# Softmax denominators of 98 attention units: turned by a DMA transpose and added up on VectorE, with PV ten slots behind

## The chip, the core and the metric

The kernel runs on one core of one Trainium2 chip. A core has TensorE (PE in the profile; its weight loads are PEld), VectorE (DVE), ScalarE (ACT), GpSimd (POOL), SyncE (SP, which here only issues transfers) and 16 DMA engines that all issuing engines share. The time is the device time of one execution in microseconds; several runs give a median.

## The reference

Inputs are bf16. `x` has 2048 tokens of width 512; attention has 32 heads of width 128 over a cache of 2048 keys and values.

```python
xn = layernorm(A_x)                                   # 2048 x 512
# attention: 32 heads, q from xn, keys and values from the cache
q = (xn @ wq) per head                                # 32 x 2048 x 128
p = softmax(q @ k_cache^T * 128**-0.5)                # 32 x 2048 x 2048
s = (p @ v_cache, heads side by side) @ wo            # 2048 x 512
# mixer and MLP on the same xn
h  = gelu(layernorm(xn) @ w1)
x1 = xn + shifted(h) @ w2      # four groups of columns, shifted by -1, +1, -2, +2 tokens
g  = silu(x1 + gelu(layernorm(x1) @ w3) @ w4)         # w3: 512 x 1792
out = A_x + s * g
```

## The kernel before

**Units and slots.** The attention is cut into 128 units: one head (`hh`, four to a group `g`) with one block of 512 queries (`qt`), in the order group, query block, head (`units`). A unit is eight slots. In slot p, `s_slot` computes the scores of two chunks of 128 keys (two matmuls of 512 columns into `ps_s`, keys on the partitions, queries along the columns) and ScalarE's exponential (line 194) writes them as bf16 into half of a `pT` tile; a tile holds two slots, and there are four. `pv_slot` runs `LAG` = 5 slots later and adds two matmuls, V times the exponentials, to the unit's accumulator `ps_o` in PSUM (`psO`, two buffers). So every slot issues two score matmuls and two PV matmuls, and other matmuls are put between them: Q of the unit after next in slots 0 and 1 (`q_mm`, copied out by `q_copy` in slot 2), the output projection of one block of 128 tokens in slots 4 and 5 (`wo_mm`, added into `s_acc` by `wo_post` in slot 6), and the mixer and MLP, cut into 136 chunks, in slots 2 and 3 and in slots 6 and 7, spread evenly from window 10 on. The mixer's first GEMM with its gelu (`m1_chunk`) takes about units 5 to 18, its second (`m2_chunk`) units 19 to 32, and then the wide MLP follows in four rounds of `m3_chunk` (gelu) and `m4_chunk` (silu).

**Denominators.** The softmax needs, for each query, the sum of the exponentials over all 2048 keys. VectorE adds a unit's four `pT` tiles: `add_first` in slot 4, `add_next` in slot 6, and in slot 0 of the next unit `add_last`, which adds the last tile and then folds the four 512-wide parts into one (lines 205, 210, 211). What remains, `acc[:, 0, :]`, has 128 partial sums per query, one per partition. `sums` in slot 3 adds across partitions on TensorE: four matmuls with `acc` as weights and a column of ones as data give a 128x4 tile in PSUM, query 4p+j at partition p, column j. VectorE's reciprocal (`recip`, line 233) writes `rc`; SP stores it to DRAM as `dr` (line 235, 16 contiguous bytes per partition); in slot 4 `bcast` (line 250) reads it back, repeated on all 128 partitions, into `rb` (`rp`, two buffers); and in slot 2 of the unit after, `norm` (line 261) multiplies `ps_o` by `rb` into `oT` and frees the accumulator.

**What sets the order.** The loop over slots writes the order out by hand, and `pin` keeps it on each engine. Each engine, and each issuing queue, works in order: what waits holds up all that is behind it. `todo` holds work for later slots (gelu steps, loads). SP issues the stores and broadcasts above, the loads of K (as transposes), V and weights, and the transposes of normalized tokens; POOL issues the loads and stores of the MLP. Tags with fixed numbers of buffers limit how far transfers run ahead: `ta` and `tb` for token tiles, `w3` for the weights of the wide MLP. PSUM has one bank with the tag `xa` (Q, sums, WO in turn) and one with `xm` (the MLP; late in the run also the sums).

**The ends.** The last group defers two token blocks of the group before it (`deferred`), and the last seven units (`QUIET`) are arranged apart; the last unit's sums are made in parts after the loop (`split_sums`).

Of the kernel before, what the change touches and what calls it, by code (L numbers as in the profile page):

```python
# [9 lines left out]
ALU = mybir.AluOpType  # L10
FP32 = mybir.dt.float32
BF16 = mybir.dt.bfloat16
# [5 lines left out]
def kernel(  # L18
# [70 lines left out]
    wqp = ent(pool("wqp", HG + 2))  # L89
    wop = ent(pool("wop", 2 * HG))  # L90
    qtp = ent(pool("qt", 4))
    ptp = ent(pool("pt", 4))
    trp = ent(pool("tr", 2))
    rp = ent(pool("rp", 2))
    otp = ent(pool("ot", 2))
    smp = ent(pool("smp", 4))
    gtp = ent(pool("gt", 2))
# [26 lines left out]
    LQ = QT - 1  # L124
    deferred = {(NG - 2, qt): qt for qt in (LQ - 1, LQ)}
    NS = NU * SPU
    kTs, vBs, wqs, wos, oTs, st = {}, {}, {}, {}, {}, {}
    todo = defaultdict(list)

    def at(n, fn):  # L130
        todo[n].append(fn)
# [42 lines left out]

    def q_copy(u):
        qT = qtp.tile([P, 512], BF16, name="qT")
        if u > QUIET + 1:
            pin(nc.scalar.activation(out=qT[:], in_=st[u].pop("psq")[:], func=ACT.Identity))
        else:
            pin(nc.vector.tensor_copy(out=qT[:], in_=st[u].pop("psq")[:]))  # L180
        st[u]["qT"] = qT
# [49 lines left out]
    def recip(s, ps):  # L231
# [2 lines left out]
        s["dr"] = drp.tile([P, 4], FP32, name="dr")  # L234
        pin(nc.sync.dma_start(out=s["dr"][:], in_=rc[:]))

    def split_sums(u, parts):
        s = st[u]
        if "ps" not in s:
            s["ps"] = psX.tile([P, 4], FP32, tag="xm", name="ps_sum")  # L240
        for a, first, last in parts:
            a = a.rearrange("k (p j) -> k j p", j=4)
            for j in range(4):
                mm(s["ps"][:, j:j + 1], a[:, j, :], ones_t[:], first and j == 0, last and j == 3)
        if parts[-1][2]:
            recip(s, s["ps"])

    def bcast(u):
        st[u]["rb"] = rp.tile([P, 512], FP32, name="rb")
        pin(nc.sync.dma_start(  # L250
            out=st[u]["rb"][:], in_=st[u]["dr"][:].rearrange("p j -> (p j)").partition_broadcast(P)))

    def norm(u, pieces=1):
        g, qt, hh = units[u]
# [58 lines left out]
    fin = {}  # L313

    def fin_load(t):
        xl = tokp.tile([P, D], BF16, tag="ta", bufs=8, name="xl")
        nc.gpsimd.dma_start(out=xl[:], in_=xsrc[t])
        gl = tokp.tile([P, D], BF16, tag="ta", bufs=8, name="gl")
        nc.gpsimd.dma_start(out=gl[:], in_=g_d[t][:])
        fin[t] = (xl, gl)  # L320

# [17 lines left out]
    ln = {}  # L339

    def ln1_load(t, eng):
        xin = tokp.tile([P, D], BF16, tag="ta", bufs=8, name="xin")
        pin(eng.dma_start(out=xin[:], in_=xsrc[t]))
        ln[t] = xin

# [11 lines left out]

    def ln1_norm(t):
        xin = ln.pop(t)
        xn = tokp.tile([P, D], BF16, tag="tb", bufs=8, name="xn")  # L360
        norm1(t, xn[:], xin[:])
        return xn

# [121 lines left out]
            lambda: hT[:, 2 * jp:2 * jp + 2, b + tt * 512: b + (tt + 1) * 512])  # L485

    def xn_load(t):
        mlp["xnext"] = tokp.tile([P, D], BF16, tag="tb", bufs=8, name="xr")
        nc.gpsimd.dma_start(out=mlp["xnext"][:], in_=xsrc[t])

    def m2_chunk(t):
# [37 lines left out]
    def ln2(c, n):  # L529
        def start():  # L530
            mlp["xn2T"] = mp.tile([P, DC, 512], BF16, name="xn2T")
            xs = []
            for ts in range(4):
                xr = tokp.tile([P, D], BF16, tag="ta", bufs=8, name="x1r")
# [12 lines left out]

        at(n, start)
        for ts in range(4):
            at(soft(n + 8 + 2 * ts), lambda ts=ts: apply(ts))  # L550

    def m3_chunk(c, fc):
        def dest():
            mlp["h2"][fc // 2] = mlp["ph2"].tile([P, 2, 512], BF16, tag="h2T", bufs=FC // 2, name="h2T")
            return mlp["h2"][fc // 2][:]

        inner = gelu_chunk(
            lambda dc: mlp["w3"][:, dc, (fc % 2) * P:(fc % 2 + 1) * P],
            lambda dc: mlp["xn2T"][:, dc, :], fc % 2, None, dest)
# [22 lines left out]
    def m4_chunk(t, part):  # L582
        fcs = list(M4[part])
        ts = t % 4

        def run(i, n):
            if part == 0 and i == 0:
                mlp["ps"] = psX.tile([P, 512], FP32, tag="xm", name="ps_m")
                mlp["xr"] = tokp.tile([P, D], BF16, tag="tb", bufs=8, name="xr")
# [24 lines left out]
        return run  # L614
# [7 lines left out]
    for t in range(NT):  # L622
        if t == 8:
            hooks[len(chunks)] = lambda n: ln2(0, n)
        if t == 12:
            hooks[len(chunks)] = lambda n: [w3_prefetch() for _ in range(3)]
        chunks.append(m2_chunk(t))
    hooks[len(chunks)] = lambda n: ph2_open()
    for c in range(QT):
# [48 lines left out]
    for g in range(NG - 1):  # L678
        b = (g * QT + QT - 1) * HG
        for hh in range(HG):  # L680
# [11 lines left out]
            at((QUIET + 1 + 2 * (t % 4)) * SPU + 4, lambda t=t: gate_sum(t))  # L692

    wo_todo = deque()
    for n in range(NS):
# [19 lines left out]
        if p == 2 and u >= 2:  # L715
            norm(u - 2)
            gg, qq, hh = units[u - 2]
            if hh == HG - 1 and (gg, qq) in deferred:
                pin(nc.sync.dma_start(out=o_d[qq][:], in_=oTs[(gg, qq)][:]))
            elif hh == HG - 1:  # L720
                wo_todo.extend((gg, 4 * qq + ts) for ts in range(4))
                if gg == NG - 1:
                    fin_load(4 * qq)
# [8 lines left out]
        if p == 6 and wo_todo:  # L732
            gg, t = wo_todo.popleft()
            wo_post(gg, t)
            if gg == NG - 1:
# [103 lines left out]
```

## Time and profile before

| what | value |
| --- | --- |
| median of 3 runs | 1280.42 us (1280.09 to 1280.76) |
| the profiled execution | 1279.53 us, its span 1277.8 us |
| TensorE clock granted | 0.999 |
| busy: PE / DVE / ACT / POOL | 1257.1 / 1019.2 / 1113.0 / 137.9 us |
| exponentials, 1024 | 1012.0 us, 1.031 us each |
| matmuls of the sums, 516 and 32 | 34.3 and 1.5 us, 0.17 us each |
| stores `dr`, 128 | 1.4 us from issue to landing (median) |
| broadcasts `rb`, 128 | 4.1 us from issue to landing (median) |

Busy time counts an instruction from its start to its end. Instructions of one engine overlap, so the sum of their lengths can be more than the time in which the engine could do them; the distance between two starts tells what one costs. A row of groups gives line, engine, operation, output and inputs, shapes and count, then the busy time and the mean of one in ns, then the engine's idle time before them and what ended it.

### The profile page before, as it was taken

What the parts mean: (1) busy time and instruction counts of PE and PEld (TensorE: products, weight loads), DVE (VectorE), ACT (ScalarE), POOL (GpSimd) and SP (SyncE); (2) the same over time, 40 slices, a digit from 0 to 9 for tenths busy, and PEclk for the clock granted to TensorE, in tenths of its full rate; (3) what the DMA queues carried; (4) which work ended last, traced back from release to release, by engine and by line L of the source; (5) the groups of instructions that cost most, each with busy time, mean ns of one, the idle gap of its engine ahead of it and who ended that gap; (6) DMA issues with size and microseconds to landing.
All of it is one profiled execution on the core that took longest, in us unless ns stands there. A gap on an engine that the chain in (4) does not pass through costs nothing.

```text
span 1277.8 us, 17233 instructions
## 1 busy us (share of the span) xinstructions
PE 1257.1 (98%) x6195; PEld 612.1 (48%) x6320; DVE 1019.2 (80%) x1407; ACT 1113.0 (87%) x1195; POOL 137.9 (11%) x241
## 2 busy tenths in 40 slices
PE   8999999999999999999999999999999999999998
PEld 5444444444444444444444444444444444444444
DVE  7888889898788877778887778887777888777886
ACT  7899998888999988899988889998888999888883
POOL 4430003323110010000001000000000000000110
PEclk9999999999999999999999999999999999999999
DMA  9644343455532564134443244523435133542532
GB/s 185 133 106 81 59 79 88 108 124 123 115 77 67 100 110 89 42 75 83 89 93 68 58 85 93 96 42 75 96 80 90 34 70 72 91 105 46 140 76 58
DMA packets 172950, 111.79 MB, mean 87 GB/s; under 512 B 124800, under 2 KB 149888, under 8 KB 172864
## 3 DMA queue, kind: packets, MB, share of 16 engines
q1 hardware_dynamic: 163904, 85.51, 34.3%
q0 software_dynamic: 8672, 24.91, 7.9%
q8 instruction: 49, 0.80, 0.3%
q14 instruction: 37, 0.30, 0.1%
q10 hardware_dynamic: 288, 0.26, 0.1%
HBM read 82.58 MB, written 7.60 MB: 71 GB/s over the span
## 4 chain that ended last, share of the span: by engine, by line
PE 87%; ACT 6%; DVE 4%; issue 1%; DMA 1%; POOL 0%; DVEq 0%; ACTq 0%
PE ps_s L114 31%; PE ps_o L114 30%; PE ps_m L114 9%; PE ps_wo L114 8%; PE ps_q L114 7%; ACT pT L194 4%; PE ps_sum L114 1%; ACT sq L425 1%; DVE acc L205 1%; ACT pre L455 1%; DVE bn L349 0%; DMA rb<-dr 0%; DMA xnT<-xn 0%; DVE acc L210 0%; DVE qT L180 0%
## 5 line engine op out<-in xcount | busy, mean ns | idle before, releaser
L194 ACT ACTIVATE pT<-ps_s 128x1024 bf16<-128x1024 f32 x1024 | 1012.0, 1031 | 141.0 <-PE ps_s L114 130.0
L114 PE MATMUL ps_s<-qT,kT 128*128 128x512 bf16 x2004 | 599.5, 379 | 4.1 <-ACT pT L194 1.0
L114 PE MATMUL ps_o<-pT,vb 128*128 128x512 bf16 x1997 | 597.6, 379 | 2.8
L205 DVE TENSOR_TENSOR acc<-acc,pT 128x2048 bf16<-128x2048 bf16 x254 | 309.8, 1220 | 65.5 <-ACT pT L194 60.8
L114 PEld LDWEIGHTS <-kT 128*128 128x128 bf16 x2048 | 226.8, 113 | 224.4 <-issue 18.6
L114 PEld LDWEIGHTS <-vb 128*128 128x128 bf16 x2048 | 199.8, 98 | 225.2
L200 DVE TENSOR_TENSOR acc<-pT 128x2048 bf16<-128x2048 bf16 x128 | 155.9, 1218 | 26.6 <-ACT pT L194 26.4
L114 PE MATMUL ps_q<-xnT,wq_h 128*128 128x512 bf16 (+1 forms) x519 | 150.7, 374 | 3.3 <-DMA xnT<-xn 2.0
L114 PE MATMUL ps_wo<-wo_h,oT 128*128 128x512 bf16 x456 | 136.3, 379 | 0.6
L328 DVE TENSOR_TENSOR s_acc<-ps_wo,s_acc 128x512 f32<-128x512 f32 x100 | 68.9, 689 | 73.9 <-PE ps_wo L114 71.0
L210 DVE TENSOR_TENSOR acc<-acc 128x1024 bf16<-128x1024 bf16 x127 | 87.9, 692 | 4.4
L261 DVE TENSOR_TENSOR oT<-ps_o,rb 128x512 bf16<-128x512 f32 x129 | 87.1, 676 | 4.1 <-DMA rb<-dr 4.0
L180 DVE CAST qT<-ps_q 128x512 bf16<-128x512 f32 x122 | 83.5, 685 | 4.8 <-PE ps_q L114 4.8
L114 PEld LDWEIGHTS <-wq_h 128*128 128x128 bf16 x524 | 50.6, 98 | 63.2 <-issue 3.6
L114 PEld LDWEIGHTS <-oT 128*128 128x128 bf16 x480 | 46.9, 98 | 57.7 <-issue 2.6
L114 PE MATMUL ps_m<-xn2T,w_sb 128*128 128x512 bf16 x222 | 66.1, 378 | 0.2
L114 PE MATMUL ps_m<-w_sb,h2T 128*128 128x512 bf16 x218 | 62.7, 379 | 0.2
L577 POOL DMA_DIRECT2D w_sb<-in_B_w_dram x28 | 21.1, 756 | 353.8 <-PE ps_m L114 328.6
L211 DVE TENSOR_TENSOR acc<-acc 128x512 bf16<-128x512 bf16 x127 | 54.0, 425 | 4.3
L233 DVE RECIPROCAL rc<-ps_sum 128x4 f32<-128x4 f32 x128 | 22.9, 179 | 40.9 <-PE ps_sum L114 40.0
L114 PEld LDWEIGHTS <-acc 128*128 128x128 bf16 x516 | 37.6, 115 | 29.6 <-issue 1.5
L609 POOL DMA_DIRECT2D g_d<-xr x16 | 8.8, 547 | 346.3 <-DVE xr L607 346.3
(74 smaller groups left out, 599.9 us busy)
## 6 DMA issues: line engine op xcount, KB each, us to landing
rb<-dr SPq DMA_DIRECT2D x128, 256.0 KB, 4.1
vb<-in_A_v_cache_dram SPq DMA_DIRECT2D x64, 256.0 KB, 4.5
w_sb<-in_B_w_dram POOLq DMA_DIRECT2D x28, 256.0 KB, 4.6
wo_h<-in_A_wo_dram SPq DMA_DIRECT2D x32, 128.0 KB, 3.9
wq_h<-in_A_wq_dram SPq DMA_DIRECT2D x28, 128.0 KB, 4.2
kT<-in_A_k_cache_dram SPq DMA_TRANSPOSE x128, 4.7
dr<-rc SPq DMA_DIRECT2D x128, 2.0 KB, 1.4
xr<-in_A_x_dram POOLq DMA_DIRECT2D x16, 128.0 KB, 3.5
```

Source lines behind the costliest of these rows:

```text
L114: pin(nc.tensor.matmul(out=out, lhsT=lhsT, rhs=rhs, start=start, stop=stop))
L180: pin(nc.vector.tensor_copy(out=qT[:], in_=st[u].pop("psq")[:]))
L194: pin(nc.scalar.activation(out=s["pT"][-1][:, jj:jj + 2, :], in_=sps[:], func=ACT.Exp, scale=SCALE))
L200: pin(nc.vector.tensor_tensor(out=s["acc"][:], in0=s["pT"][0][:], in1=s["pT"][1][:], op=ALU.add))
L205: pin(nc.vector.tensor_tensor(out=a[:], in0=a[:], in1=st[u]["pT"][i][:], op=ALU.add))
L210: pin(nc.vector.tensor_tensor(out=a[:, 0:2, :], in0=a[:, 0:2, :], in1=a[:, 2:4, :], op=ALU.add))
L211: pin(nc.vector.tensor_tensor(out=a[:, 0, :], in0=a[:, 0, :], in1=a[:, 1, :], op=ALU.add))
L233: pin(nc.vector.reciprocal(out=rc[:], in_=ps[:]))
L261: pin(nc.vector.tensor_tensor(out=oTs[(g, qt)][:, hh, c], in0=s["o"][:, c], in1=s["rb"][:, c], op=ALU.mult))
L328: pin(nc.vector.tensor_tensor(out=sa, in0=ps[:], in1=sa, op=ALU.add))
L425: pin(nc.scalar.activation(out=sq[:], in_=pre[:], func=ACT.Square, scale=GELU_A ** 0.5))
L577: pin(nc.gpsimd.dma_start(out=w[:], in_=w3_v[:, :, fc * P:(fc + 2) * P]))
```

## The change

In units T0 = 16 up to T1 - 1 = 113 (98 of 128, `turned`) the four matmuls of the sums go. In slot 3 of the next unit SP issues a DMA transpose of the folded `acc[:, 0, :]`, 128x512 bf16, within SBUF (`acc_turn`); the result `accT` has query 128c+p at partition p, block c, with its 128 partial sums side by side. In slot 0 of the unit after that VectorE reduces along them (`turned_sums`, 128x4x128 to 128x4) and takes the reciprocals. SP stores them into a DRAM tile of 4x128, which is written with a stride: four single float32 per partition, 512 bytes apart. The broadcast follows in slot 2 and `norm` at the end of slot 7, five slots later than before.

To bridge this, PV runs ten slots behind the scores in those units. `LAGS` raises the distance by one every four slots from slot 132 on (five slots have no PV), and lowers it from slot 930 on (five slots have two). Six `pT` tiles stand in for four. Space for them and for `accT` comes from `rp` (1 buffer instead of 2), the `ta` tiles (6 instead of 8), the `tb` tiles (4 instead of 8, with the first block's `xn` in a pool of its own) and `w3` (2 instead of 3, with the prefetch at the end of an odd chunk and no longer at the start of an even one). The 14 `q_copy` made in units 18 to 31 (Q of units 20 to 33) move from VectorE to ScalarE. V loads of the heads after a group's first come in slot 11 counted from their unit's start, and no longer in slot 6, and the bookkeeping after `norm` becomes the function `normed`.

```diff
-    ptp = ent(pool("pt", 4))
+    ptp = ent(pool("pt", 6))
     trp = ent(pool("tr", 2))
-    rp = ent(pool("rp", 2))
+    rp = ent(pool("rp", 1))
+    atp = ent(pool("at", 1))
...
     NS = NU * SPU
+    T0, T1 = 4 * HG, NU - 14
+    M2 = (18, 31)
+    LAGS = [(T0 * SPU + 4 * (i + 1), LAG + i) for i in range(5)] + [((T1 + 2) * SPU + 2, LAG + 5)]
+    LAGS += [((T1 + 2) * SPU + 6 + 4 * i, LAG + 4 - i) for i in range(4)] + [(NS, LAG)]
...
     def q_copy(u):
         qT = qtp.tile([P, 512], BF16, name="qT")
-        if u > QUIET + 1:
+        if u > QUIET + 1 or M2[0] <= u - 2 <= M2[1]:
             pin(nc.scalar.activation(out=qT[:], in_=st[u].pop("psq")[:], func=ACT.Identity))
...
+    def turned(u):
+        return T0 <= u < T1
+
+    def acc_turn(u):
+        s = st[u]
+        s["at"] = atp.tile([P, 4, P], BF16, name="accT")
+        pin(nc.sync.dma_start_transpose(out=s["at"][:], in_=s["acc"][:, 0, :]))
+
+    def turned_sums(u):
+        s = st[u]
+        sm = smp.tile([P, 4], FP32, name="sm")
+        pin(nc.vector.tensor_reduce(
+            out=sm[:], in_=s.pop("at")[:], axis=mybir.AxisListType.X, op=ALU.add))
+        rc = smp.tile([P, 4], FP32, name="rc")
+        pin(nc.vector.reciprocal(out=rc[:], in_=sm[:]))
+        s["dr"] = drp.tile([4, P], FP32, name="dt")
+        pin(nc.sync.dma_start(out=s["dr"][:].rearrange("j p -> p j"), in_=rc[:]))
...
     def ln1_norm(t):
         xin = ln.pop(t)
-        xn = tokp.tile([P, D], BF16, tag="tb", bufs=8, name="xn")
+        xn = ph1.tile([P, D], BF16, tag="xn", bufs=5, name="xn")
...
             if i == 0 and fc % 2 == 0:
                 mlp["w3"] = mlp["w3next"].pop((c, fc))
-                w3_prefetch()
             if i == 0 and c == 0:
                 w4_load(fc)
             inner(i, n)
+            if i == 1 and fc % 2 == 1:
+                w3_prefetch()
...
-            w = mp.tile([P, DC, 2 * P], BF16, tag="w3", bufs=3, name="w3_sb")
+            w = mp.tile([P, DC, 2 * P], BF16, tag="w3", bufs=2, name="w3_sb")
...
-                at((b - 2 + (2 * hh + i + (hh > 0))) * SPU + 6, lambda h=h, i=i: load_v(h, (i,)))
+                at((b - 2 + (2 * hh + i + (hh > 0))) * SPU + (11 if hh else 6), lambda h=h, i=i: load_v(h, (i,)))
...
     for n in range(NS):
         u, p = divmod(n, SPU)
         s_slot(u, p)
-        m = n - LAG
-        if m >= 0:
-            pv_slot(*divmod(m, SPU))
+        lag = next(v for lim, v in LAGS if n < lim)
+        while pv_done <= n - lag:
+            pv_slot(*divmod(pv_done, SPU))
+            pv_done += 1
...
+        if p == 0 and u >= 2 and turned(u - 2):
+            turned_sums(u - 2)
         if p == 0 and u >= 1:
             add_last(u - 1)
+        if p == 3 and u >= 1 and turned(u - 1):
+            acc_turn(u - 1)
+        if p == 2 and u >= 2 and turned(u - 2):
+            bcast(u - 2)
         if p == 2 and HG - 1 <= u < NU - 2:
             q_copy(u + 2)
...
+        if p == (4 if u == T1 + 2 else 2) and u >= 2 and not turned(u - 2):
+            normed(u - 2)
-        if p == 3 and u >= 1:
+        if p == 3 and u >= 1 and not turned(u - 1):
             sums(u - 1)
-        if p == 4 and u >= 1:
+        if p == 4 and u >= 1 and u != T1 + 1 and not turned(u - 1):
             bcast(u - 1)
...
         for fn in todo.pop(n, ()):
             fn()
+        if p == SPU - 1 and u >= 2 and turned(u - 2):
+            normed(u - 2)
+        if p == SPU - 1 and u == T1 + 1:
+            bcast(T1)
```

More of the change, by code (lines that the diff above doesn't have):

```diff
@@ L250, in bcast @@
         pin(nc.sync.dma_start(
-            out=st[u]["rb"][:], in_=st[u]["dr"][:].rearrange("p j -> (p j)").partition_broadcast(P)))
+            out=st[u]["rb"][:], in_=st[u]["dr"][:].rearrange("a b -> (a b)").partition_broadcast(P)))
     def norm(u, pieces=1):
@@ L315, in fin_load @@
     def fin_load(t):
-        xl = tokp.tile([P, D], BF16, tag="ta", bufs=8, name="xl")
+        xl = tokp.tile([P, D], BF16, tag="ta", bufs=6, name="xl")
         nc.gpsimd.dma_start(out=xl[:], in_=xsrc[t])
-        gl = tokp.tile([P, D], BF16, tag="ta", bufs=8, name="gl")
+        gl = tokp.tile([P, D], BF16, tag="ta", bufs=6, name="gl")
         nc.gpsimd.dma_start(out=gl[:], in_=g_d[t][:])
@@ L341, in ln1_load @@
     def ln1_load(t, eng):
-        xin = tokp.tile([P, D], BF16, tag="ta", bufs=8, name="xin")
+        xin = tokp.tile([P, D], BF16, tag="ta", bufs=6, name="xin")
         pin(eng.dma_start(out=xin[:], in_=xsrc[t]))
@@ L487, in xn_load @@
     def xn_load(t):
-        mlp["xnext"] = tokp.tile([P, D], BF16, tag="tb", bufs=8, name="xr")
+        mlp["xnext"] = tokp.tile([P, D], BF16, tag="tb", bufs=4, name="xr")
         nc.gpsimd.dma_start(out=mlp["xnext"][:], in_=xsrc[t])
@@ L533, in start @@
             for ts in range(4):
-                xr = tokp.tile([P, D], BF16, tag="ta", bufs=8, name="x1r")
+                xr = tokp.tile([P, D], BF16, tag="ta", bufs=6, name="x1r")
                 nc.gpsimd.dma_start(out=xr[:], in_=x1_d[c * 4 + ts][:])
@@ L588, in run @@
                 mlp["ps"] = psX.tile([P, 512], FP32, tag="xm", name="ps_m")
-                mlp["xr"] = tokp.tile([P, D], BF16, tag="tb", bufs=8, name="xr")
+                mlp["xr"] = tokp.tile([P, D], BF16, tag="tb", bufs=4, name="xr")
                 nc.gpsimd.dma_start(out=mlp["xr"][:], in_=x1_d[t][:])
@@ L625 @@
         if t == 12:
-            hooks[len(chunks)] = lambda n: [w3_prefetch() for _ in range(3)]
+            hooks[len(chunks)] = lambda n: [w3_prefetch() for _ in range(2)]
         chunks.append(m2_chunk(t))
@@ L694, with normed @@
     wo_todo = deque()
+    pv_done = 0
+    def normed(u):
+        norm(u)
+        gg, qq, hh = units[u]
+        if hh == HG - 1 and (gg, qq) in deferred:
+            pin(nc.sync.dma_start(out=o_d[qq][:], in_=oTs[(gg, qq)][:]))
+        elif hh == HG - 1:
+            wo_todo.extend((gg, 4 * qq + ts) for ts in range(4))
+            if gg == NG - 1:
+                fin_load(4 * qq)
     for n in range(NS):
@@ L710 @@
             q_mm(u + 2, (2 * p, 2 * p + 1))
+        if p == 0 and u >= 2 and turned(u - 2):
+            turned_sums(u - 2)
         if p == 0 and u >= 1:
             add_last(u - 1)
+        if p == 3 and u >= 1 and turned(u - 1):
+            acc_turn(u - 1)
+        if p == 2 and u >= 2 and turned(u - 2):
+            bcast(u - 2)
         if p == 2 and HG - 1 <= u < NU - 2:
             q_copy(u + 2)
[L715 to L723, printed above, removed]
-        if p == 3 and u >= 1:
+        if p == (4 if u == T1 + 2 else 2) and u >= 2 and not turned(u - 2):
+            normed(u - 2)
+        if p == 3 and u >= 1 and not turned(u - 1):
             sums(u - 1)
-        if p == 4 and u >= 1:
+        if p == 4 and u >= 1 and u != T1 + 1 and not turned(u - 1):
             bcast(u - 1)
@@ L731 @@
             add_next(u, 2)
-        if p == 6 and wo_todo:
+        if p == 6 and wo_box:
             gg, t = wo_todo.popleft()
```

## The prediction

> **What bounds the kernel now.** I read the page's shares first, then the chain that ended last, then the waits, then the timeline around one group of sums, then the stages. From the page, busy time and the chain:
>
> ```profile
> span 1277.8 us, 17233 instructions
> PE 1257.1 (98%) x6195; PEld 612.1 (48%) x6320; DVE 1019.2 (80%) x1407; ACT 1113.0 (87%) x1195; POOL 137.9 (11%) x241
> ...
> PE 87%; ACT 6%; DVE 4%; issue 1%; DMA 1%; POOL 0%; DVEq 0%; ACTq 0%
> ```
>
> TensorE is busy 98% and carries 87% of the chain. Busy shares can mislead, so the waits have to agree (who waited for whom; us in total, times, longest):
>
> ```profile
> ACT pT L194 <- PE ps_s L114: 130.0, 448, 1.1
> ...
> DVE rc L233 <- PE ps_sum L114: 40.0, 71, 1.2
> ...
> DVE oT L261 <- DMA rb<-dr: 4.0, 4, 2.0
> ```
>
> ScalarE waits for TensorE 448 times, VectorE does for the sums, and hardly anything waits for the broadcast rb. TensorE sets the pace; time goes away where its own instructions go away. One group of sums in the timeline (start, length, engine, line):
>
> ```profile
> 502.37 0.59 PE L114 MATMUL ps_o<-pT,vb 128*128 128x512 bf16 x2
> 502.58 0.39 PEld L114 LDWEIGHTS <-acc 128*128 128x128 bf16 x4
> 502.80 0.26 PE L114 MATMUL ps_sum<-ones_t,acc 128*128 128x1 bf16 x4
> ...
> 502.92 0.38 PE L114 MATMUL ps_s<-qT,kT 128*128 128x512 bf16 x1
> ...
> 503.35 0.59 PE L114 MATMUL ps_o<-pT,vb 128*128 128x512 bf16 x2
> ```
>
> Pairs of 512-column matmuls start 0.43 us apart (502.37 to 502.80, 502.92 to 503.35). The four one-column matmuls of the sums, 0.17 us each in the group row, start within 0.12 us (502.80 to 502.92), because they overlap. That, not the sum of busy time, is what a unit pays.
>
> **The change, part by part.**
>
> *Sums off TensorE.* Taken over the starts of the weight loads before and after each group, the group costs 0.130 us in the median (0.125 to 0.136 between the tenth and ninetieth percentile), and in the 98 units 16 to 113 together 12.8 us. The other 30 keep it. Gain: 12.8 us, if TensorE stays the bound. Adding up busy time instead (4 x 0.172 x 98 = 67 us) would count overlap as time.
>
> *Waits behind the sums.* The sums share the one PSUM bank "xa" with Q and WO. In eleven turned units the WO matmuls of slot 4 start 0.06 to 0.16 us late, since recip stands behind a gelu step on VectorE; 1.0 us in all. With no sums in that bank this goes: 1.0 us gained (bounds 0 and 1.0; WO then waits for q_copy, which VectorE ends before the gelu step).
>
> *The reduction on VectorE.* Nearest row: one pass over 128x512 in bf16 that leaves a few numbers per partition. The reciprocal stays (0.18 us).
>
> ```profile
> L349 DVE BATCH_NORM_STATS2 bn<-xin 128x6 f32<-128x512 bf16 x16 | 10.9, 680 | 2.6 <-DMA xin<-in_A_x_dram 2.6
> ```
>
> I take 0.68 us (bounds 0.43, the 128x512 bf16 add of L211, and 0.69, the float32 write of L328): 98 x 0.68 = 67 us. What hides it is VectorE's free time, by stage (the columns of each row: stretch, its length, and busy time of each engine):
>
> ```profile
> 183.00:320.00 137.00, 136.21 (x669) 66.52 (x681) 123.59 (x197) 113.65 (x116) 42.71 (x78) 1.00 0.48 108
> 320.00:430.00 110.00, 109.30 (x532) 52.68 (x541) 88.63 (x112) 102.92 (x115) 11.55 (x19) 1.00 0.38 84
> 430.00:540.00 110.00, 109.31 (x536) 53.25 (x546) 81.82 (x113) 91.77 (x96) 7.21 (x13) 1.00 0.47 89
> ```
>
> In the first row (second part of the MLP's first block) VectorE is at 90%; 14 units add 9.5 us and 14 q_copy of 0.685 us move to ScalarE, 9.6 us: still 90%. In the second (first GEMM of the wide MLP), 88.6 + 11.3 x 0.68 = 96.3 of about 108.6: 89%. In the third, 82%. If that cover is gone VectorE becomes the bound (a rival). Within a unit turned_sums stands first in slot 0, ahead of add_last, which today finds VectorE idle (1.17 us at 498.87) until the last exponential ends, so most of it falls into that hole. Behind it wait add_last, then q_copy, which must end before WO's matmuls in slot 4: q_copy ended at 501.96, WO began at 503.79, slack 1.8 us. Cost: 0.
>
> *The chain of transfers.* Per turned unit SP now issues the store of rc (slot 0), the broadcast (slot 2) and a transpose (slot 3), before V, K and weight loads. From the issue list, median us from issue to landing:
>
> ```profile
> rb<-dr SPq DMA_DIRECT2D x128, 256.0 KB, 4.1
> ...
> dr<-rc SPq DMA_DIRECT2D x128, 2.0 KB, 1.4
> ...
> xn2T<-x1r SPq DMA_TRANSPOSE x16, 3.8
> ```
>
> The added transpose has xn2T's form (128x512 bf16, SBUF to SBUF), 2.4 to 5.8 us. The store writes 4-byte pieces, 512 instead of 128; no store of before is like it. The present one's 16-byte packets take 9 ns, eight per DMA engine; 32 would add 24 x 0.009 = 0.2 us. Bounds: 1.4 (as now) and 4 x 1.4 = 5.6 us; I take 2, nearer the packets. Then, from the start of a unit: reduce and reciprocal 0.9, store 2.9, broadcast lands at 7.0; norm is due at slot 7 (8.4 us) and its psO buffer at slot 2 of the next unit (12 us). The accumulator is done at about 3.3, the transpose lands at 7.1; it is needed at 9.6. V, K and weight loads get 1.5 us later on SP and are due units later. Where K and V load at the same time a landing can slip by 2 us (K's spread is 2.6 to 7.0), which the slack holds. Cost: bounds 0 and 54 loading units x 0.1 us; I take 0.5 us.
>
> *PV ten slots behind.* Six tiles cover twelve slots, so the exponential of slot n reuses a tile whose PV (n-11) was issued ahead of the scores it waits for anyway: 0. In slots 132 to 148 five PV pairs are skipped, 5 x 0.43 = 2.15 us of TensorE work put off; if ScalarE can't go faster there TensorE idles, and the work is made up in units 116 to 118, so the cost is between 0 and 2.15 us. ScalarE's exponentials can start 0.92 us apart (three in 2.86 us where merged) and its gelu steps 0.95 (start to start), which leaves it about 0.8 us per unit in those 2.5 units, 2.0 against 2.15: I take 0.5.
>
> *ScalarE bursts.* Within units 17 to 116 TensorE loses 8.3 us to waits of 0.04 to 0.56 us at the scores, nearly all after gelu steps. Removing sums helps only if ScalarE has been idle since the group; in six of the 98 units it hasn't, so 6 x 0.13 = 0.8 us are lost. In units 18 and 19 q_copy, 0.59 us in ScalarE's row of L178, meets the last gelu steps of the first block: 0 to 2 x 0.6; 0.3.
>
> *Smaller pools and moved loads.* rp with one buffer makes a broadcast wait for the norm before it, which ends at least two slots earlier. w3 with two buffers is fetched two windows (about 10 us) ahead and lands in 4.6; POOL waits less, as the matmuls that free the buffer are already issued. Six "ta" tiles make POOL wait for first_tokens before loading tokens 6 and 7, which are used some 10 us later; V at slot 11 starts after the old head's PV. Each 0, bounds plus or minus 0.5 for the start.
>
> Sum: 12.8 + 1.0 - 0.5 - 0.5 - 0.8 - 0.3 = 11.7 us. The profiled execution took 1279.5 (span 1277.8) and becomes 1267.8; the median of the runs, 1280.4, stands 0.9 above it, so 1268.7, said as 1269.
>
> **The rivals.** 0.2% (2.6 us) is about what a measurement of this kernel can tell from no change.
>
> *The transfer loop becomes the bound (slower).* SP waits in order: the transpose stands behind the broadcast, which waits for the store, which waits for the reduction, which waits for the previous transpose. One turn of this loop is store + 0.3 + 3.8 + 0.9 = store + 5.0, and it must fit in a unit of 9.6. It decides from a store of 4.6 us on; each 0.1 beyond costs 98 x 0.1 = 9.8 us. At the upper bound of 5.6 us that is 98 us, less the 12: 1366. For it: the store's four strided elements per partition. Against: 9 ns packets and stores that landed by 4.3 us at worst. The Trainium skill, DMA: Bandwidth & Descriptors, in Rules for kernel authors, speaks against the change here: a non-contiguous last dimension becomes one descriptor per element. By that rule the store has 512 descriptors; no run here shows what they take, and only a price above 4.6 us would turn the sign. Chance 8%.
>
> *VectorE becomes the bound.* In-order waits (for exponentials, WO, two landings) could make 90% into more than it can hold. If it lost 0.2 us in each of 98 units, 20 us come back: 1289. Units with two gelu steps show it first (9.13 of 9.84 us busy; with 0.68 it is 9.8 against 9.7), their neighbours at 7.3 have room. It decides when more than 0.12 us a unit is lost. Chance 6%.
>
> *Half hidden.* Late landings in loading units and ScalarE's bursts give back a third to two thirds: 1272 to 1277. Chance 14%.
>
> *ScalarE is the real bound.* Then nothing comes of it: 1280. Its 130 us of waiting for TensorE speak against it. Chance 5%.
>
> **The numbers.** Likeliest case 67%: 1269, own range 1266.5 to 1272. Range over the cases: 1266 to 1281, which leaves out the two slower ones (14%) and some 4% below. Faster 81%, within 0.2% 5%, slower 14%.
>
> **What would show it.** 156 sum matmuls instead of 548 (4 x 29, and 40 for the last unit), scores following PV at 0.43 us in turned units; a reduction of about 0.68 us x98 with little idle time before it; the 4-byte store landing by 3 us; PE waits at the scores within 1 us of 8.3; VectorE near 85%. I am wrong if the reduction or norm waits for landings in most units, or if units 17 to 116 have not become 0.12 us shorter each.

## The result, and the profile after

The changed kernel takes 1939.34 us in the median (1938.32 to 1943.9, 4 runs) against 1280.26 us before (1280.05 to 1280.76, 4 runs): 1.5154 times as long, 95% interval 1.5128 to 1.518. The forecast was 1269 us with a range of 1266 to 1281. It is wrong by 670 us, in the direction of the rival that was given 8%.

The page of the changed kernel, span, shares and chain:

```profile
span 1937.2 us, 16635 instructions
...
PE 1457.3 (75%) x5928; PEld 638.7 (33%) x5928; DVE 1070.9 (55%) x1491; ACT 1132.7 (58%) x1209; POOL 139.3 (7%) x241
...
DMA 76%; PE 11%; DVE 10%; SPq 1%; issue 1%; ACT 1%; POOL 0%; DVEq 0%
DMA dt<-rc 49%; DMA rb<-dt 20%; DMA accT<-acc 6%; PE ps_s L115 4%; PE ps_o L115 4%; DVE sm L253 3%; DVE oT L284 3%; PE ps_wo L115 1%; DVE acc L210 1%; PE ps_q L115 1%; DVE rc L256 1%; PE ps_m L115 1%; ACT pT L199 1%; SPq L273 0%; DVE acc L215 0%
```

TensorE carried 87% of the chain and now carries 11%. Transfers carry 76%, and nearly half of the whole span is one of them: the store of the reciprocals. Its landing and its neighbours', from the issue list (last figure: median us from issue to landing):

```profile
rb<-dt SPq DMA_DIRECT2D x98, 256.0 KB, 5.3
...
accT<-acc SPq DMA_TRANSPOSE x98, 5.4
dt<-rc SPq DMA_DIRECT2D x98, 2.0 KB, 9.1
```

The store lands after 8.3 to 12.6 us. The forecast took 2 and allowed 5.6. Who waits (us in total, times, longest), first on the engines, then on SP's queue:

```profile
DVE oT L284 <- DMA rb<-dt: 655.3, 98, 11.1
...
PE ps_o L115 <- DVE oT L284: 456.4, 98, 10.4
```

```profile
SPq L273 <- DMA dt<-rc: 913.2, 98, 12.2
SPq L258 <- DVE rc L256: 263.4, 89, 6.3
```

The first line alone has the size of the whole loss: in each of the 98 units `norm` waits for the broadcast, 6.7 us on average. One turn on SP's queue in the timeline (start, length, then what is issued):

```profile
944.16 0.33 SPq L273 DMA_DIRECT2D rb<-dt  x1
944.59 1.22 SPq L248 DMA_TRANSPOSE accT<-acc  x1
...
950.95 0.36 SPq L258 DMA_DIRECT2D dt<-rc  x1
959.89 0.33 SPq L273 DMA_DIRECT2D rb<-dt  x1
```

From one broadcast to the next 15.7 us pass: 6.8 from the broadcast to the next store (it lands, `norm`, reduction, reciprocal) and 8.9 for the store to land. Over all 98 the transposes are issued 16.6 us apart (178.8 to 1786.4 us in 97 steps). The sum by medians is 9.1 + 0.3 + 5.3 + 0.7 + 0.9 = 16.3. The granted clock fell to 0.862 in a run in which TensorE is busy for 75% of the span; with 11% of the chain on it, that explains little.

The part that was costed by a row came out as costed:

```profile
L253 DVE TENSOR_REDUCE sm<-accT 128x4 f32<-128x512 bf16 x98 | 66.6, 680 | 9.7 <-DMA accT<-acc 9.5
```

### The profile page after: what moved, and what is told of

Same layout as the page of the kernel before. It is cut to its first block, busy times and chain, and to the rows that moved or that the text cites. A ratio compares the mean times of both kernels' runs of the same rounds, so it can differ in the third digit from the quotient of the medians.

```text
span 1937.2 us, 16635 instructions
## 1 busy us (share of the span) xinstructions
PE 1457.3 (75%) x5928; PEld 638.7 (33%) x5928; DVE 1070.9 (55%) x1491; ACT 1132.7 (58%) x1209; POOL 139.3 (7%) x241
## 4 chain that ended last, share of the span: by engine, by line
DMA 76%; PE 11%; DVE 10%; SPq 1%; issue 1%; ACT 1%; POOL 0%; DVEq 0%
DMA dt<-rc 49%; DMA rb<-dt 20%; DMA accT<-acc 6%; PE ps_s L115 4%; PE ps_o L115 4%; DVE sm L253 3%; DVE oT L284 3%; PE ps_wo L115 1%; DVE acc L210 1%; PE ps_q L115 1%; DVE rc L256 1%; PE ps_m L115 1%; ACT pT L199 1%; SPq L273 0%; DVE acc L215 0%
## 5 line engine op out<-in xcount | busy, mean ns | idle before, releaser
L115 PE MATMUL ps_o<-pT,vb 128*128 128x512 bf16 x2048 | 695.5, 426 | 456.4 <-DVE oT L284 456.4
L115 PE MATMUL ps_s<-qT,kT 128*128 128x512 bf16 x2048 | 676.3, 415 | 1.7 <-ACT pT L199 1.0
L115 PEld LDWEIGHTS <-vb 128*128 128x128 bf16 x2048 | 214.5, 105 | 745.9 <-issue 564.7
L115 PEld LDWEIGHTS <-kT 128*128 128x128 bf16 x2048 | 241.8, 119 | 288.1 <-issue 109.4
L205 DVE TENSOR_TENSOR acc<-pT 128x2048 bf16<-128x2048 bf16 x128 | 155.8, 1217 | 14.8 <-ACT pT L199 14.3
L115 PE MATMUL ps_m<-xn2T,w_sb 128*128 128x512 bf16 x224 | 88.1, 484 | 0.0
L115 PE MATMUL ps_m<-w_sb,h2T 128*128 128x512 bf16 x224 | 81.2, 464 | 0.0
L185 DVE CAST qT<-ps_q 128x512 bf16<-128x512 f32 x108 | 73.8, 683 | 5.3 <-PE ps_q L115 5.3
L253 DVE TENSOR_REDUCE sm<-accT 128x4 f32<-128x512 bf16 x98 | 66.6, 680 | 9.7 <-DMA accT<-acc 9.5
L478 ACT ACTIVATE pre<-ps_m 128x512 bf16<-128x512 f32 x72 | 42.9, 596 | 15.2 <-PE ps_m L115 14.7
L115 PEld LDWEIGHTS <-w_sb 128*128 128x128 bf16 x288 | 32.9, 116 | 48.6 <-issue 28.6
```

The lines of the kernel that those rows point to most:

```text
L115: pin(nc.tensor.matmul(out=out, lhsT=lhsT, rhs=rhs, start=start, stop=stop))
L205: pin(nc.vector.tensor_tensor(out=s["acc"][:], in0=s["pT"][0][:], in1=s["pT"][1][:], op=ALU.add))
L253: pin(nc.vector.tensor_reduce(out=sm[:], in_=s.pop("at")[:], axis=mybir.AxisListType.X, op=ALU.add))
L478: pin(nc.scalar.activation(out=pre[:, j, :], in_=mlp["ps"][:], func=ACT.Identity))
```

## The experiments

Two questions were open: is it the store alone, and why is it slow; and what would the change have given with a store that lands in time. The kernel before, timed beside these runs on the same chips, stayed between 1279.4 and 1280.8 us in the median.

### The store in whole pieces

```diff
-        s["dr"] = drp.tile([4, P], FP32, name="dt")
-        pin(nc.sync.dma_start(out=s["dr"][:].rearrange("j p -> p j"), in_=rc[:]))
+        s["dr"] = drp.tile([P, 4], FP32, name="dt")
+        pin(nc.sync.dma_start(out=s["dr"][:], in_=rc[:]))
...
+            v = "q (j p) -> q j p"                       # norm, turned units
+            pin(nc.vector.tensor_tensor(
+                out=oTs[(g, qt)][:, hh, :].rearrange(v, j=4), in0=s["o"][:].rearrange(v, j=4),
+                in1=s["rb"][:].rearrange("q (p j) -> q j p", j=4), op=ALU.mult))
```

> The changed kernel with one thing different: the reciprocals are stored as 128 pieces of 16 contiguous bytes, and norm reads rb with a stride instead (query 128c+p at place 4p+c). Theory (the single-float store, 9.1 us from issue to landing, stretches the loop sums, store, broadcast, norm to 16.5 us): the store lands in 1.4 to 2 us as before, the loop takes about 9 us and fits in a unit, and the time is 1269 us (1266 to 1275), with norm's mean still near 0.69 us. Rival (the transposes, or three transfers per unit in SP's order, or norm at slot 7, are what holds VectorE up): norm goes on waiting several us in every unit and the time stays above 1600 us.

Measured: 1279.98 us, 0.9996 of before (0.9987 to 1.0005). From its issue list:

```profile
rb<-dt SPq DMA_DIRECT2D x98, 256.0 KB, 4.3
...
dt<-rc SPq DMA_DIRECT2D x98, 2.0 KB, 1.4
```

All 660 us hang on the form of the store; transposes, SP's order and the late `norm` hold up nothing on that scale. But 1269 us was missed too: the kernel is merely as fast as before, and `norm` takes 1.07 us, not 0.69. The later runs look for these 11 us.

### The store alone

```diff
 # kernel before, units 16 to 113: sums stay on TensorE
-        a = s["acc"][:, 0, :].rearrange("k (p j) -> k j p", j=4)
+        a = s["acc"][:, 0, :].rearrange("k (j p) -> k j p" if single else "k (p j) -> k j p", j=4)
...
+            s["dr"] = drp.tile([4, P], FP32, name="dt")
+            pin(nc.sync.dma_start(out=s["dr"][:].rearrange("j p -> p j"), in_=rc[:]))
```

> The kernel before with only the store changed in units 16 to 113: the sums stay on TensorE (weights taken so that query 128j+p comes to partition p, column j), PV stays five slots behind, no transposes; rc is written as 512 single floats. Theory: the loop reciprocal 0.2, store 9.1, broadcast 0.3 + 4.5 to 5.3, norm 0.7 closes on VectorE, whose norm of the unit before stands ahead of the next reciprocal: 14.8 to 15.6 us per unit in place of 9.75, so 1280 + 98 x 5.05 to 5.85 = 1775 to 1855 us. Rival (the transposes and the traffic they add make the store slow): the store lands in 2 to 4 us here and the time stays under 1300 us.

Measured: 1891.24 us, 1.4767 of before (1.4740 to 1.4794), with neither transposes nor reductions. The store lands in 9.1 us here too, and `norm` waits (first the issue list, then the waits):

```profile
rb<-dt SPq DMA_DIRECT2D x98, 256.0 KB, 5.5
...
dt<-rc SPq DMA_DIRECT2D x98, 2.0 KB, 9.1
```

```profile
DVE oT L266 <- DMA rb<-dt: 533.1, 98, 9.2
...
PE ps_wo L114 <- DVE rc L234: 362.9, 85, 8.4
```

It is 36 us over the upper end of what was expected; with the broadcast's 5.5 us and stores that landed 1 us later in a quarter of the units (upper quartile 10.1 us) the loop is 16 us instead of 14.8 to 15.6; from one store's issue to the next the trace has 16.1.

### What makes the store slow

The kernel before with extra stores that nobody waits for, from a tile of their own.

```diff
+    pB = prd.tile([4, P], FP32, name="pB_4B_turned")     # one of the eight layouts
...
+    probes = [(pA[:], pz[:]), (pB[:].rearrange("j p -> p j"), pz[:]), (pC[:, :, 0], pz[:]),
...
+        pin(nc.sync.dma_start(out=probes[i][0], in_=probes[i][1]))
...
+    for u in range(20, 116):
+        at(u * SPU + 6, lambda u=u: probe(u % 8))
```

> The kernel before, unchanged, plus one store per unit in units 20 to 115 that nobody waits for, from a tile of its own, in eight layouts in turn. It measures what a store costs by its layout. Theory (each separate piece written to DRAM costs its share, whatever its place): landing grows with the number of pieces, 128 pieces 1.4 us (16 bytes contiguous, 16 bytes each in a 64-byte field of its own, or a single float per partition), 256 pieces of 8 bytes about 4 us, 512 pieces of 4 bytes about 9 us (turned, 8 bytes apart, or each in a field of 64 bytes). Rival one (neighbouring pieces collide because different partitions write into one 64-byte field): 512 pieces in fields of their own land in 2 to 3 us, the turned ones in 9. Rival two (the cost lies at DRAM, not in the transfer): the same 512 pieces into SBUF land in 2 to 3 us. The total stays within 5 us of 1280.

Three of its eight layouts, from the issue list (12 stores each):

```profile
pH_4B_one<-pz SPq DMA_DIRECT2D x12, 0.5 KB, 10.0
...
pB_4B_turned<-pz SPq DMA_DIRECT2D x12, 2.0 KB, 11.1
pC_4B_own<-pz SPq DMA_DIRECT2D x12, 2.0 KB, 4.3
```

The theory of a price per piece falls: 512 floats in 64-byte fields of their own (`pC`) land in 4.3 us, 128 single floats side by side (`pH`) take 10.0. The first rival's order holds, though `pC` lands in 4.3 us and not in 2 to 3. The other layouts: 16 contiguous bytes 3.2 us, 16 bytes each in 64 bytes 3.7, 512 floats into SBUF 4.1, 8 bytes apart 6.5, pieces of 8 bytes turned 5.9.

These landings have a floor that is not the store's own. In these kernels transfers land nearly in the order of their issue: in the kernel before, 130 were issued while a broadcast had 3 us or more to go, and all landed behind it; behind a transpose of K it was 72 of 82. The probes stand behind a broadcast or a load, and those of 16 bytes and those into SBUF mostly landed 0.2 to 0.4 us behind it. The slow layouts stand clear: every `pH` landed 4.7 us or more behind what was ahead. `pC` took 4.0 and 4.2 us the two times that what stood ahead had landed within 1.1 us.

The run, a single one, took 1335.98 us, 55 more than before and not within 5: what is issued behind a slow store lands late as well (`dr` 2.4 us in the median instead of 1.4, at worst 9.9). All 12 `dr` issued while a turned store was under way landed behind it, nine of them within 0.6 us. This is not confined to SP's queue. In the run with the store alone, 58 transfers were issued while a slow store had 3 us or more to go, 50 of them by POOL, and all 58 landed behind it.

A second run tried the distance alone, in units without K and V loads:

> The kernel before, unchanged, plus 24 stores that nobody waits for, in units without K and V loads: one float per partition 4, 8, 16, 32 and 64 bytes apart, the four turned floats, four floats per partition 16 bytes apart, and 16 bytes in one piece. Theory (writes that fall into the same 64 bytes of DRAM wait for one another, about half a us each, and the number of pieces does not matter): 16 writes per 64 bytes (4 bytes apart, and the turned ones) land in 9 to 11 us, 8 writes in 5 to 6, 4 writes (16 bytes apart, four 16 bytes apart, one piece of 16) in 1.5 to 3.5, fewer the same. Rival (single floats are slow as such): one float per partition takes the same time at every distance.

Landing in us, median of three stores each, from the trace:

```
one float per partition,  4 bytes apart (16 in 64 bytes)   9.1
one float per partition,  8 bytes apart ( 8 in 64 bytes)   5.1
one float per partition, 16 bytes apart ( 4 in 64 bytes)   3.5
one float per partition, 32 bytes apart ( 2 in 64 bytes)   4.3
one float per partition, 64 bytes apart ( 1 in 64 bytes)   4.1
four floats turned, as in the change    (16 in 64 bytes)  10.0
four floats, 16 bytes apart             ( 4 in 64 bytes)   4.2
16 bytes in one piece                   ( 4 in 64 bytes)   3.2
```

The price goes with the number of writes that fall close together, (9.1 - 5.1) / 8 = 0.5 us for each from eight to sixteen. Below that these stores don't tell: all twelve of the rows for 16, 32 and 64 bytes apart and for one piece landed 0.15 to 0.19 us behind the broadcast or load ahead of them, so these four figures are upper bounds. How large the field is, 64 bytes or another size, these layouts can't tell. The packets don't show it: of the store at 1001.0 us in the changed kernel the last 4-byte packet begins 1.3 us after the issue, and the landing comes at 9.2. That the writes wait for one another at the memory is what fits; it was not seen directly.

### The loop taken apart

The changed kernel, slow store kept, three lines moved.

```diff
-        if p == 0 and u >= 2 and turned(u - 2):
-            turned_sums(u - 2)
...
-        if p == 3 and u >= 1 and turned(u - 1):
+        if p == 2 and u >= 1 and turned(u - 1):
             acc_turn(u - 1)
...
+        if p == SPU - 1 and u >= 1 and turned(u - 1):
+            turned_sums(u - 1)
         if p == SPU - 1 and u >= 2 and turned(u - 2):
             normed(u - 2)
```

> The changed kernel with the slow store kept and three lines moved: the transpose of a unit is issued ahead of the broadcast on SP, and the reduction of a unit stands ahead of the norm of the unit before it on VectorE (both in slot 7). Theory (an in-order loop with one turn per unit sets the time, not the traffic): the turn now spans two units: store 9.1, broadcast 5.6, norm 0.7, then the last add 2.3, transpose 5.4, reduction 0.9, 24 us for two, 12 us per unit in place of 16.5, so 1269 + 98 x 2.4 = about 1500 us (1450 to 1570). Rival (what is slow is the traffic itself, which loads the transfer engines): the same work is done, and the time stays above 1850 us.

Measured: 1782.51 us, 1.3918 of before (1.3893 to 1.3944). With the same transfers 157 us come back, so the order is part of the bound; 440 were expected. Neither range was met. What was missed is that a slow store holds up what is issued behind it: the transposes now land in 7.5 us (5.4 in the changed kernel) and the stores in 10.9 (9.1), medians of the 63 and 58 whose landing the trace has. All 43 transposes issued while a store had 3 us or more to go landed behind it. With these figures 10.9 + 0.4 + 5.2 + 0.7 + 2.3 + 7.5 + 0.9 = 27.9 us for two units is 14 per unit; in the trace the transposes are issued 14.8 us apart.

### The start

In the run with whole pieces unit 0 begins 2.3 us late and unit 7 3.5 us late. POOL's timeline there:

```profile
4.60 0.61 POOL L518 DMA_DIRECT2D xr<-in_A_x_dram  x1
5.24 0.58 POOL L120 TENSOR_TENSOR rs<-ve,nhalf 128x1 f32<-128x1 f32 x1
...
7.37 0.62 POOL L518 DMA_DIRECT2D xr<-in_A_x_dram  x1
```

Loads that are due 180 us later stand between the first tokens' rsqrt steps.

```diff
-        nc.gpsimd.dma_start(out=mlp["xnext"][:], in_=xsrc[t])
+        pin(nc.gpsimd.dma_start(out=mlp["xnext"][:], in_=xsrc[t]))
```

> The kernel with the contiguous store (16 bytes per partition) and one more word: the load of the next token tile for the mixer's second GEMM is kept in program order. In the run with the contiguous store unit 0 begins 2.3 us late and unit 7 3.5 us late, and four of these loads stand between POOL's rsqrt steps in the first 10 us. Theory: the smaller pools gave these unordered loads a free buffer at the start, they were moved to the front of POOL, and the first tokens waited: unit 7 starts within 0.5 us of the kernel before, and the time falls from 1280.0 by about 3.4, to 1276.5 us (1275.5 to 1277.5). Rival (six token tiles make POOL wait at the start): unit 7 stays 3 us late and the time stays at 1280.

Measured: unit 7 starts as before (0.05 us earlier), and the time is 1278.24 us, 0.9990 of before (0.9981 to 1.0000). The cause of the late start is shown, but the time lies above the range, and in the profiles only 0.9 of the 3.5 us are left at the end (spans 1277.4 and 1276.5): 1.9 go in units 29 and 30, where PV now waits for a late broadcast, and 0.6 after unit 116.

### The two prices, each by itself

Without the reduction:

```diff
-            out=sm[:], in_=s.pop("at")[:], axis=mybir.AxisListType.X, op=ALU.add))
-        rc = smp.tile([P, 4], FP32, name="rc")
-        pin(nc.vector.reciprocal(out=rc[:], in_=sm[:]))
+        pin(nc.vector.reciprocal(out=rc[:], in_=s.pop("at")[:, 0, 0:4]))
```

> The kernel with the contiguous store and the ordered load, without the reduction in units 16 to 113: the reciprocal reads four elements of accT, so VectorE is spared 0.68 us per unit and the denominators are left out there; transposes, store, broadcast, norm and PV's distance stay. Theory (the 12.8 us taken from TensorE come back as waits behind a VectorE that is late: q_copy behind the reduction, WO's matmuls behind q_copy): these waits, some 6 us, go, and the time is about 1270 us (1268.5 to 1272). Rival (ScalarE's gelu steps take the gain, or the transfers do): 1276 us, within 1.5 of the same kernel with the reduction.

Measured: 1272.45 us, 0.9939 of before (0.9926 to 0.9953), 5.8 less than with it and 0.5 above the range. The waits of WO's matmuls, read from the starts of weight loads in units 16 to 116 (0.216 us apart behind a 512-column matmul that waited for nothing; what is over is wait), fall from 6.7 us to 0.3. In unit 34 with the reduction (timeline; in brackets the engine's idle time and what ended it):

```profile
337.99 1.22 DVE L466 SCALAR_TENSOR_TENSOR h2T<-sq,pre 128x1024 bf16<-128x1024 bf16 x1
...
340.12 0.67 DVE L253 TENSOR_REDUCE sm<-accT 128x4 f32<-128x512 bf16 x1
...
342.88 0.42 DVE L216 TENSOR_TENSOR acc<-acc 128x512 bf16<-128x512 bf16 x1
...
343.22 0.68 DVE L185 CAST qT<-ps_q 128x512 bf16<-128x512 f32 x1
...
343.96 0.59 PE L115 MATMUL ps_wo<-wo_h,oT 128*128 128x512 bf16 x2 [0.25 <-DVE qT L185]
```

A late gelu step of the unit before (line 466) pushes `norm`, reduction and last add back until `q_copy` ends after WO is due.

The kernel before without the sums:

```diff
+        if 16 <= u < NU - 14:
+            recip(s, s["acc"][:, 0, 0:4])
+            return
```

> The kernel before, with nothing changed but that units 16 to 113 leave out the four matmuls of the sums; the reciprocal reads four elements of the folded accumulator in place of the sums. It measures what the sums cost where they were. Theory (TensorE is the bound and the starts of its weight loads show 0.13 us per group): 12.8 us less and up to 1 us of WO waits, 1267 us (1266 to 1269). Rival (ScalarE's bursts are nearly as tight a bound, so that time taken from TensorE turns into waits for exponentials): less than 7 us come of it, 1273 us or more.

Measured: 1269.35 us, 0.9915 of before (0.9901 to 0.9928) and 0.4 above the range; in the profiles 11.1 us less of span. TensorE gives 12.8, the WO waits 1.0, and the waits at the scores grow from 7.0 to 9.7 us in units 22 to 116: 12.8 + 1.0 - 2.8 = 11.0.

### The change as it was meant

The stride in `norm` came in with the repair. Without it, the put-right of the queries' order left out:

```diff
 # the kernel with whole pieces and ordered load; norm as in the change
-        if turned(u):
...
-                in1=s["rb"][:].rearrange("q (p j) -> q j p", j=4), op=ALU.mult))
-            return
         w = 512 // pieces
...
                 out=oTs[(g, qt)][:, hh, c], in0=s["o"][:, c], in1=s["rb"][:, c], op=ALU.mult))
```

> The kernel with the contiguous store and the ordered load, but norm reads rb straight, without the stride. The put-right of the queries' order is left out, so that the factors go to wrong queries there; every instruction and transfer is otherwise the same. In the run with the stride norm took 1.07 us in place of 0.69. This is the change as it was forecast, with a store that lands in 1.4 us. Theory (VectorE's lateness is what costs, 0.68 us for the reduction and 0.38 us for the stride): the WO waits fall from 6.7 to 2 us or less, and the time from 1278.2 to 1273.5 us (1272.5 to 1275). Rival (the reduction's place ahead of q_copy is what costs, whatever norm takes): the WO waits stay above 5 us and the time above 1277.

Measured: 1274.19 us, 0.9952 of before (0.9939 to 0.9965). The WO waits are 0.3 us in units 22 to 116 and 0.6 in all from 16 on. So VectorE had room for the reduction but not for the reduction and the stride, and the change with a store that lands in 1.4 us is worth 6.4 us, not 11.7.

### A version that beats both

`q_copy` first, then the norm of the unit three back, then the reduction; PV twelve slots behind; seven exponential tiles:

```diff
-    T0, T1 = 4 * HG, NU - 14
+    T0, T1 = 5 * HG, NU - 14
...
         if p == 2 and HG - 1 <= u < NU - 2:
             q_copy(u + 2)
+        if p == 2 and u >= 3 and turned(u - 3):
+            normed(u - 3)
+        if p == 2 and u >= 2 and turned(u - 2):
+            turned_sums(u - 2)
```

> The kernel with the contiguous store and the ordered load, with VectorE's work in another order: q_copy first in slot 2, behind it the norm of the unit three back, then the reduction of the unit two back; PV twelve slots behind and seven exponential tiles (space from smaller token and weight pools), and the rise of PV's distance begins in unit 20, outside the first block's gelu (94 turned units). Theory (what takes the gain is that q_copy, which WO's matmuls wait for, stands behind the reduction): the WO waits, about 5 us between units 22 and 116, and 1.5 us of the waits in units 16 to 22 go, 0.5 us is lost with the four units: 1270.5 us (1269 to 1273), faster than the kernel before by some 10 us. Rival (VectorE's total is what counts, or ScalarE's bursts do): the waits only move, to the scores or to PV's buffers, and the time is 1275 to 1278 us.

Measured: 1275.66 us, 0.9959 of before (0.9946 to 0.9973). That is in the rival's range, and the waits did move: those of WO are gone (0.04 us), and 4.4 us of waits for `norm` came in their place, 2.6 of them in units 23 and 29. The profiled run also lost 2.1 us near 35 us, where after a wait of 2.6 us the clock was granted at 0.64 and 0.50 for some 4 us; in the kernel before a wait of 2.3 us in the same place left it at 1.00. The next run took that loss for one of the smaller pools:

```diff
-        if p == 2 and u >= 3 and turned(u - 3):
+        if p == 1 and u >= 3 and turned(u - 3):     # ahead of q_copy; PV eleven behind, before the scores
             normed(u - 3)
```

> As the kernel with norm later, with the pools as they were before that (six exponential tiles, six Q weights): PV eleven slots behind and put ahead of the scores within a slot, norm of the unit three back in slot 1 between the last add and q_copy, the reduction behind q_copy in slot 2. 94 turned units. Theory (the start of the run with norm later lost 2.5 us to its smaller pools, and its order of VectorE is what saved the WO waits): unit 7 starts within 0.3 us of the kernel before, WO waits stay under 1 us, and the time is 2.5 us less than that run's 1275.7, 1273 us (1271.5 to 1274.5). Rival (norm in slot 1 comes too late for the accumulator that PV needs in slot 3): TensorE waits 0.1 us or more for it in most units and the time is 1276 us or more.

Measured: 1348.25 us, 1.0537 of before (1.0523 to 1.0552). The rival came true, in 93 of 94 units:

```profile
PE ps_o L115 <- DVE oT L283: 67.3, 93, 1.3
```

Its expectation was also wrong about the pools: the next run has the small ones again and starts unit 7 only 0.3 us late. Last, the twelve-slot version with the stride where it costs nothing:

```diff
-            v = "q (j p) -> q j p"
+            v = "q (p j) -> q p j"                       # norm writes oT and reads rb in order
...
-                out=oTs[(g, qt)][:, hh, :].rearrange(v, j=4), in0=s["o"][:].rearrange(v, j=4),
-                in1=s["rb"][:].rearrange("q (p j) -> q j p", j=4), op=ALU.mult))
+                out=oTs[(g, qt)][:, hh, :].rearrange(v, j=4), in0=s["o"][:].rearrange("q (j p) -> q p j", j=4),
+                in1=s["rb"][:].rearrange(v, j=4), op=ALU.mult))
...
+                o = oT[:, hh, :].rearrange("d (p j) -> d j p", j=4)[:, ts, :]    # WO's weights
```

> The kernel with norm later (PV twelve slots behind, reduction behind q_copy), with the stride moved: norm writes oT and reads rb in order and reads ps_o in PSUM with a stride, and WO takes its weights from oT with a stride. 92 turned units (20 to 111). Theory (a stride over float32 in SBUF is what makes norm 1.07 us; TensorE's strided weights cost nothing, as those of the sums did at 0.115 us a load): norm takes 0.69 us, PV's waits for norm (4.4 us) fall by half, and the time is 1273.5 us (1272 to 1275). Rival (any stride of this kind costs, wherever it is): norm stays at 1.0 us or more and the time within 1 us of 1275.7.

Measured: 1272.08 us, 0.9940 of before (0.9929 to 0.9952), 8.5 us faster than the kernel before and 667 faster than the change. `norm` in its group row is back at 681 ns:

```profile
L283 DVE TENSOR_TENSOR oT<-ps_o,rb 128x512 bf16<-128x512 f32 x92 | 62.7, 681 | 2.6 <-DMA rb<-dt 2.6
```

WO's strided weight loads take 112 ns instead of 98, beside running matmuls. PV's waits for `norm` are 2.3 us, about half. Not all of the gain over the first twelve-slot run is the stride's: of the 4.9 us between the two profiles 2.2 lie at the start, where the clock stayed at 1.00 this time.

## Why the prediction was wrong

**The step that failed** is the one on the chain of transfers: "The present one's 16-byte packets take 9 ns, eight per DMA engine; 32 would add 24 x 0.009 = 0.2 us. Bounds: 1.4 (as now) and 4 x 1.4 = 5.6 us; I take 2, nearer the packets." Packet time is the time on the transfer engine, and landing is something else: the packets did end within 1.3 us. No row of before bounded the store from above. The factor of four was a count of pieces; the runs show that crowding counts for more: 512 pieces in fields of their own land in 4.3 us, 128 crowded ones in 9 to 10. The Trainium skill's rule in DMA: Bandwidth & Descriptors, Rules for kernel authors, that a non-contiguous last dimension becomes one descriptor per element, was weighed and given 8%. It pointed at the right transfer, and the trace agrees (512 four-byte packets per store); it gives no price.

**The rival's mechanism** was nearly right. The loop exists; the store took 9.1 us, and (9.1 - 4.6) x 98 = 441 us was the price by its own formula. (The unit was taken as 9.6 us; in the trace of before units 18 to 114 take 9.9 each, so the break-even lay nearer 4.9; that the stores took 9.7 us in the mean works the other way.) The other 218 are 2.2 us per turn, which the path accounts for: the loop closes over the broadcast and `norm`, which stands ahead of the next reduction on VectorE (0.3 + 5.3 + 0.7), and not over the transpose (0.3 + 3.8), and the broadcast itself lands 1.2 us later than before. The text named that order on SP, and on VectorE only what waits behind the reduction, not what it waits behind.

**Sums off TensorE**, 12.8 us, and the waits behind them, 1.0 us: right (the run without sums).

**ScalarE bursts**, 0.8 us lost: mis-sized; 2.8 us in the run without sums. The 8.3 us that it started from also hold the WO waits: by the starts of weight loads, units 17 to 116 have 7.2 us at the scores and 1.0 at WO.

**The reduction**, 0.68 us and cost 0: both held with a straight `norm` (0.68 us, WO waits 0.6 us). The slack was smaller than the one unit shown made it look: 0.38 us more per unit, from the stride, and 6 us were lost.

**PV ten slots behind**, 0.5 us, with 0.3 for `q_copy` on ScalarE: mis-sized. In units 16 to 22 waits are 2.0 us in the run with the straight norm, 0.5 in the kernel without sums: 1.5 for the two terms together. The largest two, 0.65 and 0.49 us, are waits for exponentials in unit 18, the first beside a gelu step, the second right behind a `q_copy` on ScalarE; the runs don't divide them further.

**Landings in loading units**, 0.5 us: 2.5 us with the straight `norm`, in two waits of PV for a late broadcast, in units 29 and 30; K, V and weight loads were issued just ahead of the first.

**The start**, 0 with bounds of 0.5: 3.4 us, and by a way not thought of. A smaller pool had freed a buffer for loads that no order held, and they went to the front of POOL.

In sum the store decided the sign. Without it 6.4 of the 11.7 us are left in the medians, 5.4 in the two profiled executions. By the starts of weight loads, these 5.4 are the 12.8 of the sums and 0.3 at WO, less 2.5 at the scores and 2.5 for late broadcasts in units 22 to 116, 1.3 at the scores in units 16 to 22, 0.3 at Q, 0.3 at the start and 1.1 after unit 116, where the forecast had no term: 5.1.

## What to carry to other kernels

Price a transfer by landings of the same layout at its destination; neither the packets' time nor their number bounds it, and what stands ahead of it can hide its own price. A chain that runs once per unit over in-order queues is a loop: add up one turn with what each engine has ahead of it, and compare it with the unit before anything else, since every tenth of a microsecond over the unit is paid in each. When a pool shrinks, look for instructions that no order holds: they move.

## What was not expected of the hardware

- Single floats written side by side to DRAM from 128 partitions land after 9 to 10 us; spread over 16 bytes or more they landed right behind the transfer ahead, after 3.5 to 4.3.
- A slow store delays the landings of what is issued behind it, from POOL as from SP: plain 16-byte stores went from 1.4 to 2.4 us in the median and up to 9.9.
- A 128x512 product on VectorE takes 1.07 us when its float32 operand in SBUF is read 16 bytes apart, and 0.68 when the strided operand is the one in PSUM, read 512 bytes apart.
- After a wait of TensorE of 2.3 us the granted clock stayed at 1.00 in one profile, and after 2.6 us it fell to 0.50 in another, 2.1 us lost.
